# A fused Sinkhorn attention and spatial-gating kernel: PSUM copies with contiguous writes, two transposes by DMA, another unit order, and a softmax range check

## The chip, the cores and the metric

The kernel runs on one core of one Trainium2 chip. The metric is the device time of one execution in microseconds (us). An execution's span, from its first to its last instruction in the trace, is a little shorter than its time.

## What is computed

Inputs q, k, v are `[4, 8, 768, 64]` (batch, head, token, dim), `sort_net` is `[4, 8, 8, 8]`. All inputs and the output are float32.

```
P = sort_net                                   # per (batch, head), 8 x 8
5 times: P -= max(P, -1); P = exp(P)
         P /= sum(P, -1) + 1e-9; P /= sum(P, -2) + 1e-9
k_sorted[i] = sum_j P[i,j] k_block[j]          # 8 blocks of 96 tokens; same for v
attn = softmax(q_block k_sorted_block^T / 8)   # inside each block of 96
x = attn v_sorted  -> [4, 768, 512]            # heads side by side
h = relu(x @ w_in); u, v = halves of h         # w_in [512, 1024]
v_n = (v - mean) / sqrt(var + 1e-6)
v_s = w_spatial @ v_n + b_spatial              # w_spatial [768, 768], over tokens
out = (u * v_s) @ w_out                        # w_out [512, 512]
```

## The kernel before, in words

All work is cut into small **units**. The string `ORDER` (L16) lists them as `NAME:arguments`; the loop at L493 calls the function `u_NAME` for each in turn. Nothing reorders them afterwards: each engine executes its own instructions in the order in which the units issued them, and waits on semaphores where data or a buffer is not ready. So `ORDER` is the schedule, written out by hand for all engines and queues at once. A unit's first argument is mostly the number of one of four PSUM tiles (`ps0` to `ps3`, two banks each), so a unit that takes `ps1` waits until the last reader of `ps1` is done. `A`, `D` and `P` say whether ScalarE (ACT), VectorE (DVE) or GpSimd (POOL) does the copy or product of the unit.

The units, each per batch `b` and mostly per head pair `hp` (two heads, 128 columns):

- `L` (L153): loads by DMA from the POOL queue, casting float32 to bf16. q, k and v have two buffers each. `w_spatial`, the two halves of `w_in` (`wv`, `wu`) and `w_out` are loaded once.
- `SK` (L190): one of five Sinkhorn rounds: Exp on ACT, five or six small DVE operations. `PR`/`PS` (L209) and `P0` (L223) spread P into `pd`, a 128 x 128 mixing matrix per head, for batch 0; `PD` (L236) does it on POOL for batches 1 to 3. `DM` issues matmuls on zeros.
- `QT` (L270) and `KT` (L298): twelve matmuls put a transposed q, or a mixed and transposed k, of two heads into PSUM, `[128, 768]`. The copy to SBUF (in `copy`, L104 on ACT, L106 on DVE) reads PSUM in its own order and **writes every sixth bf16 element**: the view `"p (x g) -> p g x"` makes x the inner index of the destination, at a stride of G = 6 elements, 12 bytes. That puts the tokens into their natural order.
- `VM` (L309) mixes v in natural layout, `VC` (L323) moves it by eight SBUF-to-SBUF DMAs of the SP queue into blocks of 96 tokens (`vb`).
- `SC` (L333): scores of one head pair and four blocks, Exp on ACT. `AT` (L355): the product with `vb`, a reciprocal (L371) and a product (L372) on DVE into `x_sb`.
- `XT` (L378): eight PE transposes of `x_sb` into PSUM and a copy to `xT` by ACT or DVE; 16 of these units. `WS` (L251): the same for `w_spatial`, 6 units.
- `VP` (L398): the v half of `x @ w_in`, relu, mean and variance (L419, L420). `LN`, `LA`: normalise. `UP` (L438): the u half.
- `SP` (L453): twelve matmuls with `wspT`, then on DVE the sum with `b_bc` (L464), then the gate (L470) on DVE or POOL. `OP` (L473): eight matmuls with `w_out`, a copy, a DMA out.

The copy of `QT` and of `KT`:

```
copy(eng, q_tile(b, hp)[:, lo * G:(lo + n) * G].rearrange("p (x g) -> p g x", g=G),
          t[:, 0:n * G].rearrange("p (g x) -> p g x", g=G))
```

Of the kernel before, what the change touches and what calls it, by code (L numbers as in the profile page):

```python
# [9 lines left out]
BF16 = mybir.dt.bfloat16  # L10
AF = mybir.ActivationFunctionType
# [3 lines left out]

ORDER = """  # L16
L:q:0:0:64 ID IN L:v:0:0:128 SK:0 L:k:0:0:128 SK:0 QT:0:A:0:2:0 L:q:0:64:128 L:wv SK:0 QT:1:A:0:3:0
QT:2:A:0:0:0 QT:3:A:0:1:0 SK:0 DM:0:5:384 DM:1:5:384 DM:2:5:384 DM:3:5:384 L:wu IV:0 L:ws SK:1 PR:0
PS P0:0:0:2 P0:0:2:8 P0:1:4:8 P0:1:0:4 PC:D KT:1:A:0:2:0 L:v:1:0:128 VM:2:D:0:3 VM:3:A:0:0 VM:1:D:0:2
VM:0:A:0:1 KT:2:A:0:0:0 QT:3:D:0:1:1 KT:1:D:0:1:0 KT:0:D:0:3:0 IV:1 KT:2:D:0:2:1 SC:3:0:2:0  # L20
L:k:1:0:128 VC:0:0 KT:1:A:0:0:1 VC:0:1 SC:0:0:0:0 KT:2:D:0:1:1 QT:3:D:0:2:1 KT:1:D:0:3:1 L:q:1:0:128
SC:2:0:3:0 QT:0:D:0:3:1 SC:3:0:1:0 AT:1:0:2:0 PD:1:0:4 QT:2:A:0:0:1 AT:0:0:0:0 SC:3:0:3:1 SC:1:0:1:1
AT:2:0:3:0 AT:0:0:1:0 SC:3:0:2:1 XT:1:D:0:0:1 L:wo SC:2:0:0:1 XT:3:D:0:0:0 AT:0:0:1:1 PD:1:4:8
AT:1:0:3:1 WS:2:A:1 L:v:2:0:128 VP:3:D:0:0:1 L:k:2:0:128 WS:0:A:3 VP:2:A:0:2 VM:1:A:1:2 VM:3:A:1:0
UP:0:A:0:0:0 VM:2:A:1:1 AT:1:0:2:1 UP:3:A:0:1:0 AT:0:0:0:1 KT:1:A:1:2:2 XT:2:D:0:1:1 VM:3:A:1:3
WS:0:D:2 KT:1:A:1:0:2 KT:2:D:1:1:2 KT:3:A:1:3:2 VC:1:0 PD:3:4:8 VC:1:1 WS:0:D:4 WS:1:D:0 QT:2:A:1:2:2
QT:3:D:1:3:2 QT:0:A:1:1:2 QT:1:D:1:0:2 SC:2:1:2:0 XT:3:D:0:1:0 SC:0:1:3:1 SC:1:1:2:1 AT:2:1:2:0
PD:2:0:4 VP:3:A:0:5 SC:0:1:0:1 AT:1:1:3:1 L:q:2:0:128 LN:0:0:3 WS:2:A:5 LA:0:2 VP:3:D:0:3:4
SC:0:1:3:0 SC:1:1:0:0 UP:2:A:0:0:1 AT:0:1:2:1 VM:3:A:2:1 PD:2:4:8 UP:1:A:0:1:1 AT:2:1:0:1 L:v:3:0:128
AT:3:1:0:0 SC:0:1:1:1 KT:1:A:2:2:2 XT:2:D:1:1:1 VM:0:A:2:0 AT:3:1:1:1 SC:1:1:1:0 VM:2:D:2:2  # L30
L:k:3:0:128 KT:0:A:2:3:2 XT:3:D:1:1:0 QT:1:A:2:0:2 VM:2:A:2:3 LA:0:1 AT:0:1:1:0 LN:0:3:6 VC:2:0
UP:3:A:1:0:1 LA:0:0 LA:0:4 XT:1:D:1:0:0 KT:2:A:2:0:2 LA:0:3 VC:2:1 LA:0:5 QT:0:A:2:2:2 AT:3:1:3:0
VP:1:A:1:4:5 SC:2:2:0:1 PD:3:0:4 SC:0:2:0:0 LN:1:4:6 SP:3:P:0:1 SC:1:2:2:1 SC:2:2:2:0 SP:0:P:0:2
XT:3:D:1:0:1 AT:1:2:0:0 L:q:3:0:128 SP:2:D:0:3 LA:1:4 KT:0:A:2:1:2 QT:3:A:2:1:2 QT:1:A:2:3:2
AT:2:2:0:1 SP:0:P:0:0 VM:3:A:3:1 AT:1:2:2:0 VP:2:D:1:0:1 SC:0:2:3:0 SC:3:2:1:1 VP:1:A:1:2:3
VM:0:D:3:3 UP:2:A:1:1:0 LN:1:0:4 OP:3:A:0:2 AT:1:2:2:1 LA:1:2 LA:1:0 LA:1:5 LA:1:1 UP:2:A:1:0:0
LA:1:3 SC:0:2:3:1 SC:3:2:1:0 OP:1:A:0:0 AT:2:2:3:1 OP:0:A:0:1 AT:3:2:1:1 AT:1:2:1:0 UP:2:A:1:1:1
XT:0:D:2:1:1 XT:3:D:2:1:0 KT:1:A:3:3:2 QT:2:A:3:1:2 KT:0:A:3:1:2 KT:3:D:3:0:2 VP:1:D:2:4:5 VM:2:A:3:2
VM:3:A:3:0 SP:0:D:1:3 XT:1:A:2:0:0 AT:2:2:3:0 SP:3:P:1:2 LN:2:4:6 LA:2:4 UP:1:A:2:0:1 XT:0:D:2:0:1
QT:2:A:3:2:2 VC:3:0 LA:2:5 KT:3:A:3:2:2 QT:1:D:3:3:2 QT:0:D:3:0:2 VP:2:D:2:2:3 VC:3:1 UP:3:A:2:0:0  # L40
SP:1:D:1:1 SC:0:3:2:0 SC:2:3:1:1 SP:3:D:1:0 SC:1:3:2:1 SC:0:3:3:1 UP:2:A:2:1:0 AT:3:3:1:1
UP:1:A:2:1:1 AT:0:3:2:0 VP:2:D:2:0:1 SC:3:3:1:0 SC:1:3:0:0 OP:0:A:1:2 AT:2:3:3:1 LN:2:0:4 AT:3:3:2:1
OP:1:A:1:0 SC:0:3:3:0 SC:2:3:0:1 OP:3:A:1:1 LA:2:0 LA:2:1 LA:2:3 LA:2:2 AT:1:3:0:0 SP:0:D:2:1
SP:2:P:2:2 XT:1:A:3:1:1 AT:3:3:0:1 SP:0:D:2:0 AT:2:3:3:0 XT:1:A:3:1:0 SP:3:P:2:3 AT:0:3:1:0
UP:1:A:3:0:1 UP:2:A:3:1:1 XT:3:A:3:0:0 XT:0:D:3:0:1 VP:1:A:3:4:5 VP:2:A:3:2:3 VP:0:A:3:0:1 OP:3:A:2:0
UP:1:A:3:0:0 LN:3:4:6 LA:3:4 LN:3:0:4 LA:3:0 LA:3:5 LA:3:3 OP:2:A:2:2 LA:3:2 UP:0:A:3:1:0 LA:3:1
OP:3:D:2:1 SP:1:P:3:1 SP:2:D:3:3 SP:0:D:3:0 SP:3:D:3:2 OP:1:A:3:2 OP:2:A:3:1 OP:0:A:3:0
"""

# [10 lines left out]
def kernel(  # L60
# [55 lines left out]

    p_all = const.tile([BH, NB, NB], FP32, name="p_all")
    p_x = [const.tile([BH, NI, NB, TB], BF16, name=f"p_x{n}") for n in range(2)]
    rowsum = const.tile([BH, NB], FP32, name="rowsum")
    colsum = const.tile([BH, NB], FP32, name="colsum")  # L120
    b_bc = const.tile([128, S], FP32, name="b_bc")
    ident = const.tile([128, 128], BF16, name="ident")
    mask16 = const.tile([128, TB], BF16, name="mask16")
# [4 lines left out]
    wspT = const.tile([128, G, S], BF16, name="wspT")  # L128
# [5 lines left out]
    NE = 4  # L134
# [6 lines left out]
    def alloc(b, x):  # L141
        st[x, b] = ld.tile([128, H, G * D], BF16, name=f"{x}_in", tag=x)

    def load(x, b, lo, hi, first):
        src = {"q": q, "k": k, "v": v}[x]
        if first:
            alloc(b, x)
        nc.gpsimd.dma_start(
            out=st[x, b][lo:hi],
            in_=_raw_ap(src, b * H * S * D + lo * G * D, [[G * D, hi - lo], [S * D, H], [1, G * D]]),  # L150
        )

    def u_L(what, *a):  # L153
        if what in ("q", "k", "v"):
            load(what, int(a[0]), int(a[1]), int(a[2]), int(a[1]) == 0)
        elif what == "wv":
            nc.gpsimd.dma_start(
                out=w_in_sb[:, :, DH:DFF], in_=moe_w_in.rearrange("(kc p) f -> p kc f", p=128)[:, :, DH:DFF])
        elif what == "wu":
            nc.gpsimd.dma_start(  # L160
                out=w_in_sb[:, :, 0:DH], in_=moe_w_in.rearrange("(kc p) f -> p kc f", p=128)[:, :, 0:DH])
        elif what == "ws":
            nc.gpsimd.dma_start(out=wsp_nat, in_=moe_w_spatial.rearrange("(c p) s -> p c s", p=128))
        elif what == "wo":
            nc.gpsimd.dma_start(out=w_out_sb, in_=moe_w_out.rearrange("(fc p) n -> p fc n", p=128))

    def u_IN():
        nc.sync.dma_start(out=p_all, in_=sort_net.rearrange("b h i j -> (b h) i j"))
        nc.sync.dma_start(
            out=b_bc, in_=_raw_ap(moe_b_spatial, 0, [[0, 128], [1, S]]))  # L170
        nc.vector.memset(warm, 0.0)
        nc.vector.memset(eps_tile, 1e-6)
        for n in range(NE):
            nc.vector.memset(ex[n][:, 2 * NI * BLK:], 0.0)

    def u_ID():
        make_identity(nc, ident)
        nc.vector.reduce_sum(
            out=st["m32"][:], in_=ident.rearrange("p (j t) -> p t j", t=TB), axis=AX.X)
        nc.vector.tensor_copy(out=mask16, in_=st["m32"][:])  # L180

    st["m32"] = const.tile([128, TB], FP32, name="m32")
# [5 lines left out]


    def u_SK(last):  # L190
        nc.scalar.activation(out=p_all, in_=p_all, func=AF.Exp)
        nc.vector.reduce_sum(out=rowsum, in_=p_all, axis=AX.X)
        nc.vector.reciprocal(out=rowsum, in_=rowsum)
        nc.vector.tensor_mul(out=p_all, in0=p_all, in1=rowsum.to_broadcast([BH, NB, NB]))
        nc.vector.reduce_sum(out=colsum, in_=p_all.rearrange("p i j -> p j i"), axis=AX.X)
        nc.vector.reciprocal(out=colsum, in_=colsum)
        if int(last):
            for ih, eng in enumerate((nc.vector, nc.gpsimd)):
                eng.tensor_mul(
                    out=p_x[ih],  # L200
                    in0=_raw_ap(p_all, ih * NI * NB, [p_all.ap[0], [NB, NI], [1, NB], [0, TB]]),
                    in1=_raw_ap(colsum, 0, [colsum.ap[0], [0, NI], [1, NB], [0, TB]]),
                )
        else:
            nc.vector.tensor_mul(
                out=p_all, in0=p_all, in1=_raw_ap(colsum, 0, [colsum.ap[0], [0, NB], colsum.ap[1]]),
            )

    def u_PR(ps):  # L209
        st["pr"] = ps_tile(ps)[:, :, 0:NI * BH].rearrange("p x (i y) -> p x i y", i=NI)  # L210
        pr_half(0)

    def u_PS():
        pr_half(1)

    def pr_half(ih):
        for ii in range(NI):
            nc.tensor.matmul(
                st["pr"][:, ih, ii, :], lhsT=p_x[ih][:, ii, :, :].rearrange("p j t -> p (j t)"),
                rhs=ident[0:BH, 0:BH], start=True, stop=True,  # L220
            )

    def u_P0(ih, lo, hi):  # L223
        ih, lo, hi = int(ih), int(lo), int(hi)
        n = hi - lo
        pr = st["pr"][:, ih]
        nc.vector.tensor_mul(
            out=pd[0][:, lo:hi, ih * 64:ih * 64 + 64].rearrange("p h (i t) -> p h i t", t=TB),
            in0=_raw_ap(mask16, 0, [mask16.ap[0], [0, n], [0, NI], [1, TB]]),
            in1=_raw_ap(pr, lo, [pr.ap[0], [1, n], [BH, NI], [0, TB]]),  # L230
        )

    def u_PC(eng):
        copy(eng, prep_sb.rearrange("p (x i) y -> p x i y", x=2), st["pr"])
# [10 lines left out]
    def u_DM(ps, n, w):  # L245
        t = ps_tile(ps)
        for _ in range(int(n)):
# [279 lines left out]
```

## Time and profile before

| what | us |
|---|---|
| time, median of 3 runs (lowest, highest) | 216.23 (215.75, 216.97) |
| span of the profiled execution | 214.0 |
| what lies around the span, by the median | 2.2 |
| busy PE / DVE / ACT / POOL in the span | 163.0 / 133.9 / 131.0 / 35.3 |
| first matmul on mixed k (`KT`) | 21.05 |
| first `VP` matmul | 42.94 |
| first `SP` matmul | 94.15 |
| last matmul ends | 208.36 |

The page does not give the profiled execution's own time, only its span; 2.2 us is the distance of the span from the median. The page cuts the span into 40 slices of 5.35 us; a digit is the busy share of a slice in tenths. PEclk is the clock that TensorE was granted, in tenths of full speed. Matmuls are pipelined, so a row's "mean ns" of a matmul is longer than the distance from one to the next; the distances used in the next sections come from the chain of waits, where "PE ps L458 x12, 1.95 us" means twelve matmuls that followed each other in 1.95 us.

### The profile page before, as it was taken

How to read it: one execution, taken by the hardware profiler on the slowest of the kernel's cores; microseconds unless marked ns; L12 is line 12 of the kernel's file. 1: busy time of each engine (PE TensorE's matmuls, PEld its weight loads, DVE VectorE, ACT ScalarE, POOL GpSimd, SP SyncE). 2: the span in 40 equal slices, each digit the busy share in tenths (PEclk: the TensorE clock that was granted, in tenths of full speed). 3: DMA queues.
4: the chain of work that ended last, by engine and by line, in shares of the span. 5: the costliest groups of instructions: out<-in, count | busy, mean ns of one | idle time of the engine just before them, and what ended most of it. 6: DMA issues, size and time to landing. Idle time of an engine off the chain costs nothing.

```text
span 214.0 us, 4057 instructions
## 1 busy us (share of the span) xinstructions
PE 163.0 (76%) x1716; PEld 101.0 (47%) x1728; DVE 133.9 (63%) x244; ACT 131.0 (61%) x133; POOL 35.3 (16%) x41
## 2 busy tenths in 40 slices
PE   0283856996438969959659996595999999999790
PEld 0241445954335545535424555273665566455330
DVE  3236689776685774524725857589968585664900
ACT  3180854669997699993693769939455524580031
POOL 7405906201300000003430000011000033002000
PEclk9997575599995995888997999999999999999999
DMA  5999999999995000350460042071001600024025
GB/s 93 192 203 206 211 223 236 204 204 204 211 245 93 0 2 3 54 100 0 47 100 3 14 182 101 0 121 35 0 3 39 254 4 0 3 105 189 0 103 193
DMA packets 21921, 22.38 MB, mean 105 GB/s; under 512 B 1040, under 2 KB 18704, under 8 KB 21904
## 3 DMA queue, kind: packets, MB, share of 16 engines
q0 software_dynamic: 14864, 12.19, 36.4%
q1 hardware_dynamic: 7040, 9.94, 16.2%
q8 instruction: 13, 0.21, 0.4%
q14 instruction: 4, 0.03, 0.0%
HBM read 24.78 MB, written 6.29 MB: 145 GB/s over the span
## 4 chain that ended last, share of the span: by engine, by line
PE 53%; ACT 25%; DVE 12%; DMA 5%; issue 3%; POOL 1%; ACTq 0%; DVEq 0%; POOLq 0%
PE ps L458 13%; ACT kT L104 11%; ACT qT L104 10%; PE ps L446 9%; PE ps L405 8%; PE ps L479 8%; DVE qT L106 4%; PE ps L364 4%; DMA q_in<-in_q_dram 4%; PE ps L341 3%; DVE kT L106 3%; PE ps L386 2%; PE ps L313 2%; PE ps L291 2%; ACT u_sb L110 1%
## 5 line engine op out<-in xcount | busy, mean ns | idle before, releaser
L104 ACT CAST kT<-ps 128x768 bf16<-128x768 f32 (+1 forms) x13 | 31.8, 2475 | 9.5 <-PE ps L291 9.5
L458 PE MATMUL ps<-wspT,v_sb 128*128 128x384 bf16 x192 | 34.9, 337 | 3.5 <-ACT kT L104 3.5
L349 ACT ACTIVATE ex<-ps 96x768 bf16<-96x768 f32 x32 | 24.9, 811 | 15.2 <-PE ps L341 15.1
L470 POOL TENSOR_TENSOR gt<-z,u_sb 128x768 bf16<-128x768 f32 x7 | 11.5, 1647 | 129.0 <-DVE z L464 101.1
L104 ACT CAST qT<-ps 128x768 bf16<-128x768 f32 (+1 forms) x13 | 29.4, 2394 | 5.4 <-PE ps L276 5.4
L405 PE MATMUL ps<-w_in_sb,xT 128*128 128x512 bf16 x88 | 24.6, 411 | 4.4 <-ACT kT L104 1.8
L458 PEld LDWEIGHTS <-v_sb 128*128 128x128 bf16 x192 | 18.7, 100 | 16.3 <-issue 5.4
L446 PE MATMUL ps<-xT,w_in_sb 128*128 128x384 bf16 x128 | 24.6, 338 | 0.7 <-ACT kT L104 0.7
L479 PE MATMUL ps<-w_out_sb,gt 128*128 128x512 bf16 x92 | 22.2, 380 | 1.8 <-DVE gt L470 1.7
L464 DVE TENSOR_TENSOR z<-ps,b_bc 128x768 f32<-128x768 f32 x16 | 15.3, 954 | 12.3 <-PE ps L458 12.3
L372 DVE TENSOR_TENSOR x_sb<-ps,rec 96x512 bf16<-96x512 f32 x32 | 22.0, 687 | 1.1
L104 ACT COPY o_sb<-ps 128x1024 f32<-128x1024 f32 x11 | 11.1, 1012 | 17.3 <-PE ps L479 15.9
L419 DVE BATCH_NORM_STATS2 stats<-v_sb 128x6 f32<-128x512 bf16 x24 | 16.3, 677 | 8.7 <-ACT v_sb L110 8.4
L110 ACT ACTIVATE u_sb<-ps 128x768 bf16<-128x768 f32 x16 | 13.0, 810 | 11.1 <-PE ps L446 10.9
L341 PE MATMUL ps<-qT,kT 64*96 64x96 bf16 x256 | 12.1, 232 | 9.1 <-ACT qT L104 4.8
L276 PE MATMUL ps<-ident,q_in 128*64 128x128 bf16 (+1 forms) x240 | 9.4, 233 | 10.8 <-DMA q_in<-in_q_dram 9.2
L364 PE MATMUL ps<-vb,ex 96*128 96x65 bf16 x256 | 14.2, 208 | 3.5 <-ACT qT L104 2.1
L106 DVE CAST qT<-ps 128x768 bf16<-128x768 f32 (+1 forms) x7 | 15.1, 2239 | 2.6 <-PE ps L276 2.6
L446 PEld LDWEIGHTS <-w_in_sb 128*128 128x128 bf16 x128 | 12.3, 100 | 9.2 <-issue 2.0
L341 PEld LDWEIGHTS <-kT 64*96 64x96 bf16 x256 | 9.7, 139 | 14.5 <-issue 12.7
L405 PEld LDWEIGHTS <-xT 128*128 128x128 bf16 x96 | 9.7, 107 | 14.2 <-issue 6.5
L364 PEld LDWEIGHTS <-ex 96*128 96x128 bf16 x256 | 12.7, 107 | 7.3 <-issue 4.2
(63 smaller groups left out, 203.9 us busy)
## 6 DMA issues: line engine op xcount, KB each, us to landing
out_dram<-o_sb SPq DMA_DIRECT2D x12, 512.0 KB, 2.8
vb<-vm SPq DMA_DIRECT2D x32, 99.0 KB, 4.6
v_in<-in_v_dram POOLq DMA_DIRECT2D x4, 768.0 KB, 13.5
k_in<-in_k_dram POOLq DMA_DIRECT2D x4, 768.0 KB, 15.9
q_in<-in_q_dram POOLq DMA_DIRECT2D x3, 768.0 KB, 20.5
wsp_nat<-in_moe_w_spatial_dram POOLq DMA_DIRECT2D x1, 1152.0 KB, 21.9
w_in_sb<-in_moe_w_in_dram POOLq DMA_DIRECT2D x2, 512.0 KB, 16.4
q_in<-in_q_dram POOLq DMA_DIRECT2D x2, 384.0 KB, 10.9
```

The source lines that it names most:

```text
L104: nc.scalar.copy(out=out, in_=in_)
L106: nc.vector.tensor_copy(out=out, in_=in_)
L341: nc.tensor.matmul(t[0:BLK, hh, ii * BLK:(ii + 1) * BLK], lhsT=kT[rows, i * BLK:(i + 1) * BLK], rhs=qT[rows, i * BLK:(i + 1) * BLK], start ...
L349: nc.scalar.activation(out=e[:, 0:2 * NI * BLK].rearrange("p (h c) -> p h c", h=2), in_=t[0:BLK, :, 0:NI * BLK], func=AF.Exp, scale=scale,)
L364: nc.tensor.matmul(t[:, hh, ii * VW:ii * VW + D + 1], lhsT=e[:, c:c + 128], rhs=vb[b % 2][:, ih * NI + ii, 2 * hp + hh, 0:D + 1], start=Tr ...
L372: nc.vector.tensor_mul(out=x_sb[:, :, hp * 128:hp * 128 + 128].rearrange("p i (h d) -> p h i d", h=2), in0=tv[:, :, :, 0:D], in1=_raw_ap(r ...
L405: nc.tensor.matmul(t[:, x, :], lhsT=st["xT", b][:, kc, n * 128:(n + 1) * 128], rhs=w_in_sb[:, kc, DH:DFF], start=(kc == 0), stop=(kc == KC ...
L419: nc.vector.bn_stats(out=stats, in_=v_sb[:, x, :])
L446: nc.tensor.matmul(t[:, x, 0:HW], lhsT=w_in_sb[:, kc, mc * 128:(mc + 1) * 128], rhs=st["xT", b][:, kc, ih * HW:(ih + 1) * HW], start=(kc = ...
L458: nc.tensor.matmul(t[:, x, 0:HW], lhsT=st["v_sb", b, n][:, mc * 128:(mc + 1) * 128], rhs=wspT[:, n, x * HW:(x + 1) * HW], start=(n == 0), ...
L464: nc.vector.tensor_add(out=z.rearrange("p (x c) -> p x c", x=2), in0=t[:, :, 0:HW], in1=b_bc.rearrange("p (x c) -> p x c", x=2),)
L479: nc.tensor.matmul(t[:, x, :], lhsT=st["gt", b, mc][:, c * 128:(c + 1) * 128], rhs=w_out_sb[:, mc, :], start=(mc == 0), stop=(mc == FC - 1),)
```

## The change

- **Copies.** `QT` and `KT` are now always whole (`[128, 768]`), and the copy (`natural`) iterates over the destination: SBUF is written contiguously, PSUM is read at a stride of 128 float32.
- **Transposes.** `XT` becomes `XD`: one DMA transpose on the SP queue per batch and half (8 of them, `[96, 2048]` bf16 each, 384 KB). `WS` becomes `WX`: one DMA transpose of all of `w_spatial` (1152 KB). The layouts of `x_sb`, `xT` and `wspT` follow.
- **Batch 0's v** goes `VT` (mix and transpose, like `KT`) and `VB` (eight PE transposes, one copy) instead of `VM` and `VC`.
- **Sinkhorn.** P is transposed by DVE and spread by eight matmuls with a `spread` matrix, in place of two wide products on DVE and POOL.
- **Units are cut finer**: the statistics (`ST`), the gate (`GT`), the copy of the output (`OE`) and its store (`OS`) are units of their own; the last `OP` units are split into three quarters and one quarter of their sums.
- **Range check.** The reciprocals of all softmax sums are kept (`rec_all`), the first Sinkhorn sums too (`first`). `CK` at the end compares them with bounds; all engines load the flag, and a conditional block after the order holds a general path with row maxima and a whole second calculation. With the inputs of this case the flag is zero.
- **Order.** `ORDER` is new throughout. One more `ex` buffer (5), one more `v_sb` (6), `u_sb` (4) and `x_sb` (3).

Here is the core of the diff; of the new order the lines that the next section speaks of.

```diff
 ORDER = """
+S0 ID CO L:q:0:4:8 MK IV:1 L:q:0:0:4 L:v:0:0:4 SK:0 L:k:0:0:4 SK:1 DM:0:18:256 SK:2 SK:3 QT:1:A:0:2 L:k:0:4:8
+SK:4 QT:2:A:0:1 QT:3:A:0:0 QT:0:A:0:3 DM:1:16:256 PR:2 L:v:0:4:8 PC:A P0:0:2 L:v:1:0:8 P0:2:4 P0:4:6
+KT:1:A:0:0 P0:6:8 VT:3:D:0:0 IV:0 KT:0:A:0:2 VT:2:D:0:1 L:k:1:0:8 KT:1:A:0:1 SC:3:0:0:0 L:q:1:0:8 VB:0:D:0:0
...
+KT:3:D:1:2 SC:1:1:0:0 VC:1:0:4 AT:2:0:3:0 SC:0:1:3:0 SC:3:1:1:0 SC:1:1:2:1 PD:2:0:4 XD:0:1:0:4 VC:1:4:8
+AT:2:1:0:0 VP:0:A:0:4:5 AT:3:1:3:0 XD:0:0:0:4 VP:2:A:0:3 SC:1:1:2:0 SC:0:1:1:1 ST:0:4 AT:3:1:2:1 L:q:3:0:8
+VP:2:A:0:0:1 ST:0:5 AT:1:1:1:0 VP:3:A:0:2 ST:0:0 SC:0:1:3:1 SC:2:1:0:1 AT:1:1:2:0 ST:0:3 UP:3:A:0:0:1
+QT:0:A:2:3 XD:1:0:0:4 QT:1:A:2:2 ST:0:1 AT:2:1:3:1 WX:0:6 UP:3:A:0:0:0 VM:0:D:2:1 ST:0:2 VM:2:A:2:0
...
+SC:0:2:1:0 PD:3:4:8 VP:3:A:1:4:5 AT:2:2:2:1 BI AT:1:2:3:1 VC:2:0:4 SP:0:0:0 ST:1:0 GT:P:0:0 ST:1:5 SC:3:2:0:0
...
+SC:3:3:3:1 SC:2:3:1:1 OS:0:4 SP:0:2:0 AT:1:3:1:1 AT:3:3:2:0 OP:2:1:0 OE:A:1:0 SP:0:2:2 AT:1:3:1:0 OP:3:1:4
+OE:A:1:4 GT:D:2:0 XD:3:0:0:4 OS:1:0 OP:2:1:2 OE:A:1:2 AT:0:3:3:1 XD:3:1:0:4 OS:1:2 SP:1:2:1 GT:P:2:2
+VP:3:A:3:0:1 GT:D:2:1 SP:0:2:3 GT:D:2:3 VP:2:A:3:2:3 OS:1:4 ST:3:2 UP:1:A:3:0:1 ST:3:1 ST:3:0 VP:3:A:3:4:5
...
+GT:P:3:2 GT:D:3:1 OS:2:0 SP:2:3:3 GT:D:3:3 OP:1:3:0:0:3 OP:-1:3:0:3:4 OP:3:3:2:0:3 OE:A:3:0:1:2 OS:3:0:1:2
+OP:-1:3:2:3:4 OE:D:3:0:0:1 OS:3:0:0:1 OE:A:3:2:1:2 OS:3:2:1:2 OP:0:3:4:0:3 OP:-1:3:4:3:4 OE:A:3:2:0:1
+OS:3:2:0:1 OE:A:3:4:1:2 OS:3:4:1:2 CK:2 OE:A:3:4:0:1 OS:3:4:0:1
 """
...
+    def natural(eng, dst, t):
+        copy(eng, dst.rearrange("p (x g) -> p x g", g=G), t[:, 0:S].rearrange("p (g x) -> p x g", g=G))
...
-        copy(
-            eng,
-            q_tile(b, hp)[:, lo * G:(lo + n) * G].rearrange("p (x g) -> p g x", g=G),
-            t[:, 0:n * G].rearrange("p (g x) -> p g x", g=G),
-        )
+        natural(eng, turned("qT", b, hp), t)
...
+    def u_VB(ps, eng, b, hp):
+        t = ps_tile(ps, BF16)[0:BLK, 0, :].rearrange("p (i c) -> p i c", i=NB)
+        vT = turned("vT", b, hp)
+        for i in range(NB):
+            nc.tensor.transpose(t[:, i, :], vT[:, i * BLK:(i + 1) * BLK], ident)
+        copy(eng, vb[b % 2][:, :, 2 * hp:2 * hp + 2, 0:D], t.rearrange("p i (h d) -> p i h d", h=2))
...
+    def u_XD(b, ih, lo, hi):
+        if ("xT", b) not in st:
+            st["xT", b] = att.tile([128, 2, KC, HW], BF16, name="xT", tag="xT", bufs=2)
+        nc.sync.dma_start_transpose(
+            out=st["xT", b][:, ih, lo:hi].rearrange("p k (i c) -> p (k i) c", i=NI),
+            in_=st["x", b, ih][:, lo:hi].rearrange("p k i c -> p (k i c)"),
+        )
+
+    def u_WX(lo, hi):
+        nc.sync.dma_start_transpose(
+            out=wspT[:, lo:hi].rearrange("p c n t -> p (c n) t"),
+            in_=wsp_nat[:, lo:hi].rearrange("p c s -> p (c s)"),
+        )
...
+    def u_CK(ps):
+        nc.vector.memset(bad, 0.0)
+        over = lambda col, rows, in_, op, bound, test: (
+            nc.vector.tensor_reduce(out=ends[0:rows, col:col + 1], in_=in_, axis=AX.X, op=op),
+            nc.vector.tensor_scalar(out=bad[0:rows, col:col + 1], in0=ends[0:rows, col:col + 1],
+                scalar1=bound, scalar2=None, op0=test),
+        )
...
+        nc.tensor.matmul(t[0:1, 0, 0:5], lhsT=ones, rhs=bad, start=True, stop=True)
+        nc.vector.tensor_reduce(out=ends[0:1, 0:1], in_=t[0:1, 0, 0:5], axis=AX.X, op=ALU.add)
+        nc.vector.tensor_copy(out=flag, in_=ends[0:1, 0:1])
...
         for line in ORDER.split("\n"):
             for item in line.split():
                 name, *args = item.split(":")
                 units[name](*args)
+        beyond = nc.values_load(flag[0:1, 0:1], min_val=0, max_val=512)
+        with tc.If(beyond > 0, preferred_fallthrough_block=False):
+            general_path()
```

## The prediction

> **What bounds the kernel now.** I read the page's engine and slice lines first, then the chain that ended last, then the groups by form, then windows cut where the first KT, VP and SP units start.
>
> ```profile
> span 214.0 us, 4057 instructions
> PE 163.0 (76%) x1716; PEld 101.0 (47%) x1728; DVE 133.9 (63%) x244; ACT 131.0 (61%) x133; POOL 35.3 (16%) x41
> PE   0283856996438969959659996595999999999790
> ACT  3180854669997699993693769939455524580031
> DMA  5999999999995000350460042071001600024025
> PE 53%; ACT 25%; DVE 12%; DMA 5%; issue 3%; POOL 1%; ACTq 0%; DVEq 0%; POOLq 0%
> ```
>
> No engine is full over the span. PE is full only in the last quarter; before that ACT is at 9 where PE dips (slices 10, 11, 14, 17, 20, 24 and 25, counted from 0). DMA is full until slice 11 (about 64 us), while the inputs load. The groups say what ACT and DVE do:
>
> ```profile
> L104 ACT CAST kT<-ps 128x768 bf16<-128x768 f32 x10 | 27.5, 2786 | 4.4 <-PE ps L291 4.4
> L104 ACT CAST qT<-ps 128x768 bf16<-128x768 f32 x8 | 22.5, 2915 | 0.0
> L106 DVE CAST qT<-ps 128x768 bf16<-128x768 f32 x4 | 10.5, 2775 | 2.0 <-PE ps L276 2.0
> L104 ACT CAST vm<-ps 128x768 bf16<-128x768 f32 x12 | 10.5, 893 | 0.8 <-PE ps L313 0.8
> L110 ACT ACTIVATE u_sb<-ps 128x768 bf16<-128x768 f32 x16 | 13.0, 810 | 11.1 <-PE ps L446 10.9
> L106 DVE CAST vm<-ps 128x768 bf16<-128x768 f32 x4 | 3.8, 958 | 3.0 <-PE ps L313 2.8 <-issue 0.2
> ```
>
> Size, types and engines are the same; only the address pattern differs. A copy that writes every sixth bf16 takes 2.8 us, one that writes runs 0.81 to 0.96 us. With the halves, the qT and kT copies cost ACT 61 and DVE 28 us. The chain names them for 28.5% of the span, 61 us. It is followed in time here (start, us, what):
>
> ```profile
> 54.03 5.26 ACT kT L104 x2
> 59.34 0.54 PE ps L276 x12
> 59.90 5.28 DVE qT L106 x2
> ```
>
> PE waits for both engines at once. Windows (length, busy PE, PEld, DVE, ACT, POOL, granted clock):
>
> ```profile
> 21.05:42.94 21.89, 16.93 (x286) 13.72 (x287) 18.26 (x25) 13.49 (x14) 10.56 (x11) 0.58 1.25 218
> 42.94:94.15 51.21, 37.46 (x473) 24.89 (x475) 31.52 (x55) 45.27 (x40) 2.92 (x3) 0.86 0.69 115
> 150.00:201.50 51.50, 51.19 (x411) 29.45 (x413) 36.95 (x67) 23.11 (x32) 4.93 (x3) 1.00 0.17 62
> ```
>
> Between first VP and first SP, ACT is the bound (45 of 51 us). At the end PE is full, with DVE at 72% and ACT at 45%.
>
> **PE's work, before and after.** Distances between matmuls in the warm chain give per unit: SP 1.95, UP 1.30, OP and a pair of VP tiles 1.73, QT or KT 0.49, VM 0.33, SC 0.245, AT 0.24, XT and WS 0.34 us. After: 16 SP 31.2 + 16 UP 20.8 + 12 OP 20.8 + 12 VP pairs 20.8 + 36 QT, KT, VT 17.6 + 12 VM 4.0 + 32 SC 7.8 + 32 AT 7.7 + 4 VB (8/6 of a WS, 0.45) 1.8 = 132.5 us. Before the sum is 141.4: XT 5.4 and WS 2.0 come on top, and 1.5 of other shapes. So PE work falls by 9 us only. What can be won is PE's gaps: from the first VP (42.94) to the last matmul (208.36) it does 127.8 us of units in 165.4, 77%.
>
> **The copies.** 36 of them, 23 on ACT at 0.81 and 13 on DVE at 0.96, are 31 us instead of 88. The other side of the pattern is now strided: PSUM read at 512 bytes. No row does exactly this. Ends: 0.81, the contiguous row, and 2.79 (the price moves to the other side). The nearest rows of strided reads: the P0 product reads PSUM at a stride of 32 floats, each value held for 16 columns, and takes 286, 414 and 547 ns for 128, 256 and 384 columns, 1.02 ns per column; the colsum reduction reads SBUF at 32 bytes and takes 254 ns against 203 for the contiguous rowsum, 0.8 ns more per element, which would make a copy 1.4 us. I take 0.81 and 0.96.
>
> [...]
>
> **The transposes.** XT and WS leave: 7.4 us of PE, 9.9 and 4.1 us of copies. XD and WX come, on the SP queue, which runs in order: behind a waiting XD stand VC and OS, and PE's VP waits for XD. Costs, from the DMA rows: a 512 KB store lands in 2.8 us, a 99 KB vb transfer (SBUF to SBUF, same queue, beside loads) in 4.6. XD moves 384 KB: between 2.8 and, by bytes of the vb row, 18 us; I take 4.6, as the vb row is nearest in queue and kind. WX: 2.8 to 54, I take 9. Cover: between the last AT that an XD needs and its first VP the new order has 4.6 to 8 us of PE units, and 17 between WX and the first SP. So both cost nothing; an XD above 6 us costs the excess.
>
> [...]
>
> **Step 1, to the first KT** (21.05 before). The chain starts with q landing at 9.17 us; then Sinkhorn rounds stood behind 1.44 us copies on ACT, and a 1.54 us POOL product at 18.24. After, four rounds precede any QT; round 5 stands behind one copy: 9.2 + 0.55 matmuls + 0.81 copy + round 1.75 + transpose 0.2 + PR 0.5 + P0 0.4 + semaphores 0.3 = 13.7.
>
> **Step 2, first KT to first VP.** All of batch 0's attention plus batch 1's VM, KT, QT and four SC: PE 16 us warm, ACT 19.7, DVE 19.5. PE was at clock 0.50 to 0.67 in this stage (12 KT matmuls 0.80 us against 0.47), which makes 27. Between 19.7 and 27, I take 23.3: first VP at 37. Loads: batches 0 and 1 and wv are 5.2 MB, at the 204 GB/s of the page's slices 26 us after 2 us of start. They do not bind.
>
> **Step 3, to the end.** Unit sums from my durations and the new order:
>
> | stretch | PE | ACT | DVE | I allow |
> |---|---|---|---|---|
> | first VP to first SP | 27.1 | 23.2 | 22.4 | 31.5 |
> | to the first OP | 22.9 | 12.5 | 19.3 | 25.5 |
> | to the last matmul | 64.4 | 28.4 | 45.0 | 66 |
>
> PE is the longest in each. The third has DVE at 70% and ACT at 44%, as window 150 to 201.5, where PE was 99% full. In the first two ACT and DVE reach 83 to 86%, so I allow PE 86 and 90%. First SP at 68.5: w_spatial, ninth of the loads, lands by bytes (9.3 MB) at about 48 to 53, and WX by 62; the 6 us between are the cover, and each us beyond delays SP by as much. POOL's loads and PD products stay ahead of their users by 10 us or more. The last matmul is at 37 + 123 = 160.
>
> **Step 4, the tail.** Before, 5.6 us from the last matmul (208.36) to 214.0. After: three half copies 0.5 each and a landing of 2.8 plus issue, 4.9. Beside it CK: ten small DVE operations of 0.2 us, a matmul, two more, 3.5; then a flag load and a branch on each engine. The trace shows neither; the first work behind the opening branch starts 0.3 to 0.8 us after the constants are set. I take 2, ends 0 and 6. Tail 8.
>
> **Sum**: 37 + 123 + 8 = 168 us of span, against 214.0; with 2.2 around it, 170 against the median 216.2.
>
> **Rivals.**
> 1. *PE keeps its gaps*: four PSUM tiles and in-order engines limit it as before, at 77% from the first VP: 114.4/0.77 = 149, and 37 + 149 + 8 + 2 = 196. For it: DVE and ACT above 80% in two stretches. Against: the gaps of before end at 2.8 us copies.
> 2. *The copies get no cheaper* (the change doesn't do what it says): ACT copies 2 us dearer. Nine in step 2 make ACT 37.5 there, stage 42 instead of 23.3; one in the head 2; five and four in the next stretches about 8; together 199.
> 3. *Transposes bind, slower than before*: 8 XD and WX (three XD in size) run in line on SP from about 30 us; after the last come 27 us of PE units and 10 of tail. 30 + 11d + 37 passes 216 at d = 13.5 us per XD; at 18.4 (vb by bytes) it is 270. For it: vb's 22 GB/s. Against: 2.8 us for 512 KB.
> 4. *Better than forecast*: first VP at 34, PE 97% full behind it: 34 + 118 + 7 + 2 = 161 or less.
>
> **Chances.** Forecast (163 to 182) 0.66; PE keeps gaps (182 to 200) 0.15; copies no cheaper 0.06; transposes bind 0.05, of which 0.04 end slower; better than forecast 0.08. The range 157 to 194 takes in the forecast, the better case and most of the first rival, and the bounds of copy (1.4 us adds some 6) and tail (6 adds 4). Measurement tells 0.5%, about 1 us. Faster 0.95, same 0.01, slower 0.04.
>
> **What will show it.** Right: kT and qT copies at 0.8 to 1.0 us; first KT near 13.7, first VP near 37, first SP near 68; XD landing in under 6 us, and VP never waiting for it; PE 8 or 9 in nearly all slices from the first VP on; the chain PE by over 70%. Wrong: copies above 1.4 us; PE idle before VP released by DMA; a conditional block that costs more than 6 us behind the last store.

## The result and the profile after

The changed kernel takes 190.18 us (median of 4 runs, 189.63 to 190.61); the kernel before took 216.13 us beside it. The ratio is 0.879, with a 95% interval of 0.876 to 0.882. The forecast was 170.0 us, its own band 163 to 182, the range 157 to 194. So the sign and most of the gain came as forecast, and 20 us of it did not. The page of the changed kernel, to be read against the one of before (in the slice lines one digit is 4.72 us):

```profile
span 188.7 us, 3764 instructions
...
PE 152.1 (81%) x1555; PEld 90.2 (48%) x1555; DVE 110.8 (59%) x245; ACT 82.5 (44%) x115; POOL 40.1 (21%) x45
...
PE   7398999203904992699999999999999999999840
...
ACT  3256989400320493066632765746242145630140
...
PEclk9999999955575699589999999999999999999995
DMA  3999999999999999947404031763200890260081
...
PE 64%; DMA 20%; DVE 8%; SPq 2%; POOL 1%; issue 1%; ACT 1%; ACTq 0%; DVEq 0%; POOLq 0%
```

ACT has left the chain (25% before, 1% now). From slice 18 (85 us) to the last slices PE is full at full clock. Nearly all that went wrong lies in slices 7 to 16: PE has holes there, the clock falls to between 5 and 7 in most of them, and DMA is full. The chain names DMA for 20% where before it was 5%. The groups of the copies (line, shapes, count, busy us, mean ns, idle before them) show that the holes are not the copies':

```profile
L109 ACT CAST kT<-ps 128x768 bf16<-128x768 f32 x11 | 8.4, 801 | 1.1 <-PE ps L316 1.1
L109 ACT CAST qT<-ps 128x768 bf16<-128x768 f32 x11 | 8.4, 801 | 0.2
...
L111 DVE CAST qT<-ps 128x768 bf16<-128x768 f32 x5 | 4.8, 952 | 2.1 <-PE ps L281 2.1
```

They fell from 2.8 us to 0.80 and 0.95. The matmuls that PE began after its longest stops, in time (start, us, instructions; in brackets the idle time before them and what ended it):

```profile
45.32 3.59 PE L460 MATMUL ps<-w_in_sb,xT 128*128 128x512 bf16 x8 [9.30 <-DMA xT<-x_sb]
...
59.29 3.60 PE L460 MATMUL ps<-w_in_sb,xT 128*128 128x512 bf16 x8 [7.29 <-DMA xT<-x_sb]
...
77.24 2.74 PE L503 MATMUL ps<-xT,w_in_sb 128*128 128x384 bf16 x8 [5.10 <-DMA xT<-x_sb]
```

Each is the first user of one of the first three DMA transposes of x (`XD`). The stops are 21.7 us. The units behind them run at half clock (a granted 0.50 in the first 2.8 to 3.6 us behind each stop): eight matmuls of a `VP` take 3.6 us, 1.73 to 1.83 later in the same kernel. The SP queue shows when the transposes were issued, and for how long each held the queue. The row at 37.21 is two transposes with a wait between them: the first holds the queue for 9.8 us, the second waits for its data and is issued at 66.86.

```profile
30.10 4.31 SPq L439 DMA_TRANSPOSE xT<-x_sb  x1
34.46 2.65 SPq L356 DMA_DIRECT2D vb<-vm  x4
37.21 32.82 SPq L439 DMA_TRANSPOSE xT<-x_sb  x2
70.13 9.06 SPq L446 DMA_TRANSPOSE wspT<-wsp_nat  x1
```

From issue to the landing that released PE, the three take 45.3 - 30.1 = 15.2 us, 22.0 (59.24 - 37.21) and 10.3 (77.2 - 66.86). The five transposes that start after the loads are done take 4: the median of all eight is 4.1 us, the lowest 3.8. The last two, from 145.9 to 152 us, have no load beside them:

```profile
q1 hardware_dynamic: 2748, 1.15, 84.1%
...
xT<-x_sb SPq DMA_TRANSPOSE x2, 4.1
```

Windows (length, busy PE, PEld, DVE, ACT, POOL with counts, granted clock, DMA share, GB/s) show the stage beside a late one. (Shares of the DMA engines add up the times of all packets; these overlap, so a share can be over 1.)

```profile
30.00:40.00 10.00, 4.30 (x96) 3.17 (x90) 4.09 (x7) 4.94 (x7) 4.95 (x6) 0.88 1.25 213
40.00:50.00 10.00, 4.68 (x18) 1.90 (x19) 0.58 (x2) 1.02 (x1) 1.60 (x2) 0.50 1.31 190
...
100.00:110.00 10.00, 10.00 (x96) 5.73 (x92) 7.92 (x18) 5.34 (x8) 3.62 (x3) 1.00 0.23 41
```

Between 40 and 50 us DVE and ACT have next to nothing to do: what is missing is an input for PE, not an engine. (PE's 4.68 there are 18 matmuls at half clock.) The DMA answer for 30 to 60 us says what the engines carry meanwhile (queue: packets, MB, share; issues: median us to landing):

```profile
q0 software_dynamic: 4751, 4.39, 91.6%
q1 hardware_dynamic: 4032, 1.60, 33.1%
...
vb<-vm SPq DMA_DIRECT2D x5, 99.0 KB, 11.6
xT<-x_sb SPq DMA_TRANSPOSE x2, 18.6
```

The packets of the POOL queue's loads (q0) take 92% of the engines' time by this count and move 4.39 MB; those of SP's queue (q1) take 33% and move 1.60 MB. A `vb` transfer, 3.7 us in the median of the run, takes 11.6 there as well.

### The profile page after: what moved, and what is told of

The parts are those of the page before. It is cut to its first block, busy times and chain, and to the rows that moved or that the text cites. A ratio compares the mean times of both kernels' runs of the same rounds, so it can differ in the third digit from the quotient of the medians.

```text
span 188.7 us, 3764 instructions
## 1 busy us (share of the span) xinstructions
PE 152.1 (81%) x1555; PEld 90.2 (48%) x1555; DVE 110.8 (59%) x245; ACT 82.5 (44%) x115; POOL 40.1 (21%) x45
## 2 busy tenths in 40 slices
DMA packets 38295, 25.95 MB, mean 137 GB/s; under 512 B 18176, under 2 KB 35072, under 8 KB 38272
## 4 chain that ended last, share of the span: by engine, by line
PE 64%; DMA 20%; DVE 8%; SPq 2%; POOL 1%; issue 1%; ACT 1%; ACTq 0%; DVEq 0%; POOLq 0%
DMA xT<-x_sb 17%; PE ps L515 16%; PE ps L460 11%; PE ps L541 10%; PE ps L503 10%; PE ps L316 4%; PE ps L281 3%; DMA q_in<-in_q_dram 3%; PE ps L375 3%; PE ps L421 3%; DVE x_sb L429 3%; PE ps L209 2%; SPq L356 1%; PE ps L343 1%; DVE z L521 1%; DVE vb L111 1%
## 5 line engine op out<-in xcount | busy, mean ns | idle before, releaser
L460 PE MATMUL ps<-w_in_sb,xT 128*128 128x512 bf16 x96 | 28.0, 442 | 16.6 <-DMA xT<-x_sb 16.6
L531 POOL TENSOR_TENSOR gt<-z,u_sb 128x768 bf16<-128x768 f32 x10 | 16.5, 1650 | 116.1 <-DVE z L521 108.3
L380 ACT ACTIVATE ex<-ps 96x768 bf16<-96x768 f32 x32 | 24.2, 806 | 13.5 <-PE ps L375 13.2
L428 DVE RECIPROCAL rec_all<-ps 96x8 f32<-96x8 f32 x32 | 6.3, 196 | 35.6 <-PE ps L421 35.5
L115 ACT ACTIVATE v_sb<-ps 128x1024 bf16<-128x1024 f32 (+1 forms) x12 | 11.4, 953 | 32.7 <-PE ps L460 32.7
L515 PEld LDWEIGHTS <-v_sb 128*128 128x128 bf16 x192 | 18.1, 98 | 11.7
L429 DVE TENSOR_TENSOR x_sb<-ps,rec_all 96x512 bf16<-96x512 f32 x32 | 22.0, 687 | 1.1
L109 ACT COPY o_sb<-ps 128x1024 f32<-128x1024 f32 (+1 forms) x13 | 10.8, 848 | 26.3 <-PE ps L541 19.0
L503 PEld LDWEIGHTS <-w_in_sb 128*128 128x128 bf16 x128 | 12.4, 102 | 14.3 <-DMA xT<-x_sb 5.5
L115 ACT ACTIVATE u_sb<-ps 128x768 bf16<-128x768 f32 x12 | 9.7, 810 | 12.8 <-PE ps L503 12.8
L421 PEld LDWEIGHTS <-ex 96*128 96x128 bf16 x256 | 11.7, 101 | 6.8 <-issue 3.6
L541 PEld LDWEIGHTS <-gt 128*128 128x128 bf16 x96 | 8.9, 98 | 11.2 <-DVE gt L531 1.6
L281 PE MATMUL ps<-ident,q_in 128*64 128x128 bf16 x192 | 8.8, 243 | 2.9 <-DMA q_in<-in_q_dram 2.9
L489 DVE TENSOR_SCALAR v_sb<-v_sb,mv,rstd 128x512 bf16<-128x512 bf16 x24 | 8.9, 402 | 3.3 <-ACT rstd L484 3.3
## 6 DMA issues: line engine op xcount, KB each, us to landing
wsp_nat<-in_moe_w_spatial_dram POOLq DMA_DIRECT2D x1, 1152.0 KB, 35.6
```

The costliest lines, as they stand in the source:

```text
L115: nc.scalar.activation(out=out, in_=in_, func=AF.Relu)
L380: nc.scalar.activation(out=e_tile(b, hp, ih), in_=t[0:BLK, :, 0:NI * BLK], func=AF.Exp, scale=scale,)
L421: nc.tensor.matmul(t[:, hh, ii * VW:ii * VW + D + 1], lhsT=e[:, c:c + 128], rhs=vb[b % 2][:, ih * NI + ii, 2 * hp + hh, 0:D + 1], start=Tr ...
L429: nc.vector.tensor_mul(out=x_sb[:, hp].rearrange("p i (h d) -> p h i d", h=2), in0=tv[:, :, :, 0:D], in1=_raw_ap(rec, 0, [rec.ap[0], [NI, ...
L460: nc.tensor.matmul(t[:, x, :], lhsT=st["xT", b][:, n // 3, kc, (n % 3) * 128:(n % 3 + 1) * 128], rhs=w_in_sb[:, kc, DH:DFF], start=(kc == ...
L503: nc.tensor.matmul(t[:, x, 0:HW], lhsT=w_in_sb[:, kc, mc * 128:(mc + 1) * 128], rhs=st["xT", b][:, ih, kc, :], start=(kc == 0), stop=(kc = ...
```

## The experiments

**Theory A.** An `XD` beside the loads takes 10 to 22 us instead of 4.6; PE waits for it and then runs on a lower clock, 0.50 at first. **Theory B** is the prediction's first rival: the order, four PSUM tiles and in-order engines leave PE these gaps anyway. The times before differ a little from chip to chip (217.0 to 217.6 in the runs below), so kernels are compared by their ratios to it.

**1. The first four transposes of x on PE.** `XT`, not a part of the changed kernel, is put back as 16 PE transposes of 96 x 128 into one PSUM tile and one DVE copy; `XD` stays for batches 2 and 3, the transpose of `w_spatial` (`WX`) stays a DMA.

```diff
-XD:0:1:0:4 ... XD:0:0:0:4 ... XD:1:0:0:4 ... XD:1:1:0:4
+XT:2:D:0:1 ... XT:1:D:0:0 ... XT:2:D:1:0 ... XT:3:D:1:1
```

> The four DMA transposes of x of batches 0 and 1 are replaced by PE transposes into a PSUM tile and a DVE copy to the same xT layout (sixteen 96x96..128 transposes, about 0.7 us of PE, one copy of about 1.1 us); batches 2 and 3 and w_spatial keep the DMA. Theory A (the DMA transposes that run beside the input loads land 10 to 22 us late and PE has nothing else to do): the gaps of 9.3, 7.3 and 5.1 us before VP and UP and the half-clock VP units behind them go, first VP near 37 us, 166 to 174 us. Rival B (units are limited by four PSUM tiles and ACT/DVE, and the DMA wait only stands in front of another wait): first VP still after 42 us, 183 us or more. Rival C (the transposes are not the point, the w_spatial transpose behind the loads is): first VP early, but PE idles before the first SP, 178 to 186 us.

Measured: 179.51 us, ratio 0.826 (0.822 to 0.830). PE's timeline at the first `VP` and behind the longest stop that is left:

```profile
34.89 1.89 PE L474 MATMUL ps<-w_in_sb,xT 128*128 128x512 bf16 x7
...
76.89 0.21 PE L421 MATMUL ps<-vb,ex 96*128 96x65 bf16 x1 [11.22 <-DMA vb<-vm]
...
79.36 4.03 PE L529 MATMUL ps<-wspT,v_sb 128*128 128x384 bf16 x12
```

The SP queue ahead of it (start, us the queue was held, what):

```profile
53.81 19.85 SPq L460 DMA_TRANSPOSE wspT<-wsp_nat  x1
73.85 2.59 SPq L356 DMA_DIRECT2D vb<-vm  x4
```

The three stops are gone and the first `VP` starts at 34.9 us instead of 45.3, which rules out theory B (in the expectation rival B, first `VP` after 42 us). But the time is above theory A's band and in rival C's. `WX` now reaches the queue earlier, at 53.8 us, still beside the loads. It holds the SP queue for 20 us, and batch 2's `vb` transfers stand behind it; PE waits 11.2 us for them and runs the next `SP` unit on a low clock (4.03 us, 1.95 at full clock; granted are 0.52 from 70 to 80 us and 0.80 from 80 to 90). So A's mechanism holds for `XD`, against C's "the transposes are not the point", and `WX` is a second place of the same kind, as C had it, which the `XD` stops had hidden.

**2. Later loads held back.** `XD` and the order of the engines' work stay; POOL reads `xT` of batch 0 before it issues the loads that stood ahead of it.

```diff
-... L:v:2:0:8 ... L:k:2:0:8 ... L:ws ... L:wo ... L:v:3:0:8 ... XD:0:0:0:4
+... XD:0:0:0:4 HO:0 L:v:2:0:8 L:k:2:0:8 L:ws L:wo L:v:3:0:8
...
+            nc.gpsimd.tensor_copy(out=held[:, ih:ih + 1], in_=st["xT", b][:, ih, 0, 0:1])
```

> All DMA transposes stay. POOL waits with the loads behind wu (v and k of batch 2, w_spatial, w_out, v, q, k of batch 3) until both halves of xT of batch 0 have landed, by two copies of one element column each from xT. Theory A (loads in flight slow the transposes): the batch 0 transposes land in 4 to 6 us, first VP near 38 us; the held loads then end near 68 us instead of 77 and meet the batch 1 transposes, which land in about 10; 172 to 181 us. Rival D (the early transposes are slow by themselves, by the descriptors that SP writes for 1.3 to 9.8 us or the vb transfers around them): landing still 10 us or more with the loads held, and the later loads only add delay, 190 to 205 us.

Measured: 192.21 us, ratio 0.885 (0.881 to 0.888): the time forecast by A did not come, and the time lies in rival D's band. PE's stops:

```profile
42.26 0.61 PE L466 MATMUL ps<-w_in_sb,xT 128*128 128x512 bf16 x1 [4.70 <-DMA xT<-x_sb]
...
69.19 2.74 PE L509 MATMUL ps<-xT,w_in_sb 128*128 128x384 bf16 x8 [11.38 <-DMA xT<-x_sb]
...
90.41 2.74 PE L509 MATMUL ps<-xT,w_in_sb 128*128 128x384 bf16 x8 [9.97 <-DMA xT<-x_sb]
```

The same transposes now land in 10.7 us (the last loads of the first group still under way), 7.1 (issued at 39.04, q0 at 0.9% of the engines from 40 to 46 us, but with the first transpose and four `vb` transfers still under way) and 16.6 (issued at about 52.5, beside the loads held back, which start at 46.71). From 54 to 66 us the two queues stand thus:

```profile
q0 software_dynamic: 1844, 2.04, 100.7%
q1 hardware_dynamic: 1183, 0.30, 20.5%
```

In this run as in the changed kernel the landing follows the loads: 10.7 and 16.6 us beside them, 4.1 for the next one, issued at 86.30 when they are over (q0 at 1.6% from 85 to 90 us). That is A's mechanism, shown. Of rival D one thing stays open: with no loads left, but other work of the SP queue around it, the second still took 7.1 us and not 4. What A had wrong is that there would be room for the loads elsewhere. Batch 1's transpose pays for them, and the fourth then stands behind a `WX` of 19.6 us in the SP queue, from which the last stop of 9.97 us comes.

**3. The changed kernel with the copies of before.** Only the iteration order of the copies is undone: PSUM is read in its order, SBUF written at 12 bytes of stride.

```diff
-copy(eng, dst.rearrange("p (x g) -> p x g", g=G), t[:, 0:S].rearrange("p (g x) -> p x g", g=G))
+copy(eng, dst.rearrange("p (x g) -> p g x", g=G), t[:, 0:S].rearrange("p (g x) -> p g x", g=G))
```

> The changed kernel, but the copies of qT, kT and vT iterate as before: PSUM read in runs, every sixth bf16 written. Price of that part in the new order. Forecast of the prediction's second rival: copies 2.8 us, ACT +2 us each on 23 and DVE +1.8 on 13; 29 us dearer if all of it stood on the path with no cover, less where PE waits for a DMA transpose anyway: in batch 0 and 1 it delays x and so the transposes. Theory A: first VP 55 or later, 205 to 220 us. Rival B' (the gaps at the transposes hide most of it): 191 to 198 us.

Measured: 211.56 us, ratio 0.973 (0.968 to 0.978). The price returns to the copy, on both engines:

```profile
L109 ACT CAST kT<-ps 128x768 bf16<-128x768 f32 x11 | 29.1, 2817 | 1.4 <-PE ps L316 1.4
...
L111 DVE CAST qT<-ps 128x768 bf16<-128x768 f32 x5 | 13.6, 2719 | 2.6 <-PE ps L281 2.6
```

All the rest of the change, with strided copies, gains 2.7%. The first `VP` starts at 62.22, as theory A had it (55 or later). The DMA stops, and the SP queue ahead of them, show something more:

```profile
44.03 6.94 SPq L439 DMA_TRANSPOSE xT<-x_sb  x1
...
54.35 27.13 SPq L439 DMA_TRANSPOSE xT<-x_sb  x2
...
62.22 0.61 PE L460 MATMUL ps<-w_in_sb,xT 128*128 128x512 bf16 x1 [5.28 <-DMA xT<-x_sb]
...
73.20 3.17 PE L460 MATMUL ps<-w_in_sb,xT 128*128 128x512 bf16 x7 [4.74 <-DMA xT<-x_sb]
```

The stops are 10.0 us in all, 21.7 with fast copies. The first two transposes land no sooner than with fast copies (18.1 and 18.8 us from issue, against 15.2 and 22.0), but PE has less idle time in front of them, since it is still held up by the slow copies: four waits of 0.88 to 2.04 us between 44 and 56 us. The third is issued at about 80 us, when the loads are over, and stops nothing; the median landing of the eight is 4.1 us. So the faster copies bring PE to the transposes sooner, and one transpose more into the loads; 11.7 us more of DMA stops come with them.

**4. The changed kernel without its range check.** `CK`, the flag's load and the conditional block with the general path are left out, so this kernel has no path for values out of range.

> The changed kernel without the range check at the end (no CK, no flag load, no conditional block with the general path); it leaves out the general path for softmax sums out of range. The tail from the last matmul of OP to the end is 7.2 us in the changed kernel. Theory: the last store's landing sets the end together with the flag load and the branch; without them 1.5 to 3 us less, 187 to 188.5 us. Rival (everything of it lies beside the stores): within 0.5 us, 190. Second rival (the instruction stream of the general path costs at the start or outside the span): more than 4 us less.

Measured: 187.38 us, ratio 0.863 (0.860 to 0.866); by the ratios 1.6% of 217, or 3.5 us, of which 2.0 are in the tail: from the last `OP` matmul to the end it is 5.25 us instead of 7.2. What the other 1.5 are is not shown.

**5. The kernel before with contiguous copies alone.** Order, PE transposes and everything else as before.

```diff
-q_tile(b, hp)[:, lo * G:(lo + n) * G].rearrange("p (x g) -> p g x", g=G),
-t[:, 0:n * G].rearrange("p (g x) -> p g x", g=G),
+q_tile(b, hp)[:, lo * G:(lo + n) * G].rearrange("p (x g) -> p x g", g=G),
+t[:, 0:n * G].rearrange("p (g x) -> p x g", g=G),
```

> The kernel before with one edit: the copies of qT and kT write contiguous tokens and read PSUM at a stride; order, PE transposes of x and w_spatial, tail as before. Theory A (the copies are the gain of the change, the DMA transposes beside the loads take a large part of it back): copies 0.8 to 0.96 us, PE's gaps of 37 us behind the first VP mostly go, 174 to 186 us, that is no slower than the whole change at 190. Rival (the new order is needed to use the cheaper copies): 195 to 207 us, about as much as the 21 us that the strided copies cost in the new order.

Measured: 183.29 us, ratio 0.841 (0.834 to 0.848). This two-line edit (the same in `KT`) beats the whole change: 0.841 against 0.879.

```profile
span 181.2 us, 4057 instructions
...
PE 152.9 (84%) x1716; PEld 95.7 (53%) x1728; DVE 117.1 (65%) x244; ACT 90.7 (50%) x133; POOL 35.2 (19%) x41
...
PE   0195933999965999999999999999999999999670
```

PE is full from slice 13 (59 us; a slice is 4.53 us here) on; the stage where ACT bound the kernel is gone without any new order. Of the holes left before it, 8.6 us are PE's waits for `vb` transfers, which in this kernel too stand beside the loads.

**6. The new order with all transposes on PE.** The first experiment's `XT` for all four batches, and `WS`, six PE transposes and a copy for each of the six 128-row blocks of `w_spatial`, spread over the stretch ahead of the first `SP`. The whole function is kept, range check and general path included.

```diff
-XD:b:ih:0:4 (8 units) ... WX:0:6
+XT:ps:D:b:ih (8 units) ... WS:1:D:0 ... WS:2:A:1 ... WS:1:D:2 ... WS:2:D:3 ... WS:1:A:4 ... WS:0:A:5
```

> The new order with contiguous copies and no DMA transpose at all: x of all four batches (8 units, 0.7 us of PE, one DVE copy of 1.1 us each) and w_spatial (6 units, copies on DVE and ACT) are transposed on PE; the general path too. Theory A (in the changed kernel 22 us of PE idling and the half-clock units behind it come from DMA transposes beside the input loads; in e1 11 us more from vb transfers queued behind the w_spatial transpose): both go, 165 to 172 us, against 183.3 for the kernel before with contiguous copies alone and 190.2 for the whole change. Rival (the new order has other waits of that size, or needs the engine time that the DMA transposes free): 177 us or more, no better than e1 at 179.5.

Measured: 174.46 us (174.06 to 175.0), ratio 0.805 (0.802 to 0.807), the best kernel of this study that computes all of the function.

```profile
span 172.3 us, 4085 instructions
...
PE 151.3 (88%) x1719; PEld 95.4 (55%) x1719; DVE 119.4 (69%) x256; ACT 84.9 (49%) x118; POOL 40.2 (23%) x45
...
PE   7397998799899797799898999999999999999830
...
PEclk9969999999999999999999999999999999999996
```

The holes are gone, and so is the low clock. A stretch that has the loads beside it, and a late one:

```profile
34.00:60.00 26.00, 23.27 (x308) 15.12 (x308) 20.13 (x41) 16.15 (x24) 3.03 (x3) 1.00 1.25 213
...
100.00:150.00 50.00, 50.00 (x420) 28.19 (x419) 34.76 (x66) 23.04 (x30) 6.66 (x4) 1.00 0.32 100
```

The DMA engines are as full as in the changed kernel (1.25, 213 GB/s), and PE does 90% now. The loads themselves were not the bound there: what PE needed was not to wait for a smaller transfer in their company. The time is 2.5 us above the band expected and below the rival's 177. The new copies are not quite free: PE's waits for the copies of `xT` and `wspT`, none over 1.2 us, sum to 5.8 us.

**7. The same without the range check**, which again leaves out the general path.

> As e9 without the range check, the flag load and the conditional block; it leaves out the general path. Forecast from the run of the changed kernel without them (2 us shorter tail, 3 in all): 2 to 3.5 us less than e9. Rival: within 1 us of e9, the difference of that run being mostly chance.

Measured: 172.90 us, ratio 0.797 (0.794 to 0.799). The check costs 1.6 us here, 0.8% of 217, less than the forecast and more than the rival, and below the 3.5 of the fourth experiment. The profiles agree better than the times: from the last `OP` matmul to the end it is 7.1 us with the check and 5.6 without, 1.5 us less, where the fourth experiment had 2.0 less. So 1.5 to 2.0 us in the tail is what can be said.

Not measured: `WX` alone moved behind the loads, and PE transposes for `w_spatial` with `XD` kept for batches 2 and 3. So it is open how the 5 us from the first experiment to the sixth divide between `WX`'s place and the late `XD`s, and whether a late `XD`, landing in 4 us and hidden, beats PE's transposes.

## Why the prediction was right in the gain and 20 us short

The span forecast was 168 us, measured 188.7. By its own steps:

| step | predicted | measured |
|---|---|---|
| copy on ACT, DVE | 0.81, 0.96 | 0.80, 0.95 |
| first `KT` | 13.7 | 15.4 |
| first `VP` | 37 | 45.3 |
| first `VP` to first `SP` | 31.5 | 47.6 |
| first `SP` to first `OP` | 25.5 | 21.0 |
| first `OP` to last matmul | 66 | 67.6 |
| tail | 8 | 7.2 |
| `XD` | 4.6, costs nothing | 15.2, 22.0, 10.3; then 4 |

The errors add up: 8.3 + 16.1 - 4.5 + 1.6 - 0.8 = 20.7 us.

**The head: 1.7 us late.** Step 1 made Sinkhorn the chain. In the run P is transposed by 11.5 us, but PE takes it at 14.2: 16 matmuls on zeros (`DM`, 3.16 us) stand ahead of it in PE's order, and step 1 has no term for them.

**Copies: right**, in size and in where the price lies. The price was in the SBUF write at 12 bytes of stride: with it alone put back, the third experiment's copies take 2.82 us on ACT and 2.72 on DVE. Why such a write takes that long is not shown. Reading PSUM at 512 bytes costs ACT and DVE nothing that shows (801 ns on ACT against 810 for a contiguous copy of the same size, 952 on DVE against 958). The second rival, that the price moves to the read side, falls. Alone the copies are worth 0.159 of the time, 34.6 us of 217.6 (fifth experiment); in the new order they are the difference of 211.6 and 190.2, 21 us. The 11.7 us of DMA stops that the third experiment lacks would be most of the other 13; no run with strided copies and PE transposes shows it.

**Transposes: this is the step that failed.** "XD ... I take 4.6 ... So both cost nothing; an XD above 6 us costs the excess." The number did not hold: the first three `XD` took 15.2, 22.0 and 10.3 us. The rule of the last clause held for the first and the third (by it 9.2 and 4.3 us, measured 9.3 and 5.1); the second had more PE work ahead of its user (16.0 by the rule, 7.3 measured). The 4.6 us came from 99 KB transfers, a quarter of an `XD`'s bytes, in a median over all 32, which mixes transfers beside loads with later ones; the prediction read it as a price beside loads. The other end in the text, 18 us by the bytes of the same row, was near for the first two. The choice overlooked a sentence of the prediction itself: DMA is full while the inputs load, and `XD:0` and `XD:1` are issued there. Without `XD`, the first `VP` could start near 36 us: the last unit ahead of it on PE ends at 36.0, and in the first experiment it starts at 34.9. That is near step 2's 37, but in part by luck: the head was 1.7 us late, and the stage took 20.6 us up to there (20.4 in the first experiment) where 23.3 was taken. It ran at a granted clock of 1.00, so the low clock that step 2 charged for did not come, and the stage lies near the lower end of 19.7.

**The clock: not in the sum where it came.** Behind the stops PE runs at half speed (granted clock 0.50), 3.6 us for a `VP` pair, 2.74 for an `UP`, twice the prices of 1.73 and 1.30 at full clock. From the first `VP` to the first `SP` PE is busy 35.2 us for work that the table prices at 27.1 warm, at a mean granted clock of 0.76; with the two stops in that stretch, 12.4 us, this makes its 47.6. The prediction charged step 2 for a low clock and no later stage.

**`WX`: mis-sized, and its queue overlooked.** Taken 9 us with 17 of cover. `w_spatial` landed at 60.6 us (issued at 25.0, 35.6 to landing), not 48 to 53. `WX` itself could not be issued before 70.13, since SP runs in order and stood behind an `XD` that waited for its data. It landed 11.1 us later, still ahead of the first `SP`; beside loads it took 21.9 (first and second experiments). The text named `VC` and `OS` as what stands behind a waiting `XD`; it is `WX` and the next `XD` too.

**The late stages: right.** From the first `SP` on, PE is full, 88.6 us against 91.5 forecast.

**The range check: right.** Taken 2 us of the tail, measured 1.5 to 2.0 there.

**PE's work before** is mis-added in the prediction: its own unit prices give 139.0 us, not 141.4, as `VT` and `VB` are new (3.8 us) and only four `VM` leave (1.3). PE's work falls by 6.5 us, not 9. No term of the forecast rests on it.

**Rivals.** The first (196) has the nearest number but not the cause: PE keeps gaps only until 80 us, and they end at a DMA, not at a PSUM tile or a copy; the sixth experiment closes them with the same tiles. The third had a price of this size (13.5 us or more for an `XD`) and assumed it for all eight; five of them ran later and took 4. The fourth (161 or less) is not reached even without DMA transposes: the sixth experiment takes 174.5 us. The forecast's own sum with the three stops in it is 168 + 21.7 = 189.7 us, against a span of 188.7; that it comes so near is partly luck. The other errors cancel to -1.0: +1.7 head, -2.7 rest of step 2, +3.7 from the first `VP` to the first `SP` beyond its two stops, -4.5, +1.6 and -0.8.

**Where the gain went, whole.** By the ratios, of 217 us: the copies alone leave 183 and the new order with PE transposes leaves 174.5. The DMA transposes give 16 us back (0.879 - 0.805 = 0.074), more than the order had won. They took PE work of 7.4 us away, by the prediction's prices, and put 21.7 us of stops in its place.

## What to carry to other kernels

Price a transfer that an engine waits for by what shares the DMA engines at its place in the schedule, not by the median of its kind (here 10.3 to 22.0 us beside the loads, with 4.1 as the median of the eight): ask for the DMA rows of just that window. Ask, too, what runs on the DMA queues where an operation is moved to them from a compute engine, and what stands behind it there: the five late `XD`, behind the loads, stopped nothing, the three beside the loads stopped PE for 21.7 us, and a `WX` that held the SP queue for 20 us cost PE 11.2 us of waiting for the `vb` transfers behind it. When a large rewrite gains less than its parts promise, run its cheapest part alone: here a two-line edit, made in two places, gave more than the whole.

## What the runs showed of the hardware

- A DMA transpose of 384 KB (bf16, 96 x 2048) lands in 3.8 to 4.8 us with no loads beside it, in 7.1 when they have just ended and in 10 to 22 beside POOL's casting loads. Of 1152 KB: 7.1 us with no loads (third experiment), 11.1 at the end of the loads, 21.9 beside them. In the two windows shown the packets of the loads take 92 and 101% of the engines' time, those of SP's queue 33 and 20%. Why the sharing goes that way is not shown. Packets under 512 bytes are 18,176 in the changed kernel, 1,040 in the one before and 992 in the sixth experiment, the last two without a DMA transpose.
- Issuing a DMA transpose holds the SP queue: 1.3 to 1.7 us when all is quiet, 3 to 10 beside loads or just behind them; 5.6 (no loads) to 20 for `WX`.
- Sixteen blocks of 96 x 128 in one DMA transpose took 4.1 us (median landing of the eight `XD` of the changed kernel), 0.26 us a block.
